# Fused hashed attention and gated attention experts: the scale chain in a bank, signs from two-byte halves, a first pair in four-byte tiles

## The chip, the cores and the metric

The kernel runs on one core of one Trainium2 chip. The metric is the device time of one execution in microseconds (us). The engines are PE (matrix multiplication, with PEld for its weight loads), DVE (vector), ACT (scalar and activation), POOL (GpSimd) and SP, whose queue issues every DMA of this kernel.

## The reference

Two stages. Stage one is attention within hash buckets, for 4 batches of 8 heads; stage two is a gated mixture of 4 causal attention experts on what stage one returns.

```python
q_bits = (np.einsum('bhsd,dk->bhsk', q, proj) > 0)      # B, H, S, D = 4, 8, 768, 64; proj is 64 x 6
k_bits = (np.einsum('bhsd,dk->bhsk', k, proj) > 0)
mask = q_bucket[:, :, :, None] == k_bucket[:, :, None, :]   # bucket: the 6 bits as a number
scores = np.where(mask, scale * q @ k.T, -1e9)              # scale = 1 / 8
attn = exp(scores - max); attn /= attn.sum() + 1e-9
x = (attn @ v) as (B, S, H * D)
# then, for each of 4 experts e, of which the gate takes 2 per token:
a = softmax(causal(scale * (x @ wq[e]) @ (x @ wk[e]).T))
out += gate weight * (a @ (x @ wv[e]) @ wo[e])
```

## The kernel before

**Units.** The work is cut into units: ("L", b, h) is one head of stage one, ("M", b, e) one expert of stage two, 48 in all. The first eight units are the heads of batch 0; after that heads of batch b stand between experts of batch b-1. Heads come in pairs (hp), and a pair is prepared together: 16 pairs.

**One head.** `max_steps` multiplies queries by keys into the bank `mx`, nine chunks of up to 512 columns, and DVE takes the maxima of each into `pm`. `shift_steps` folds them to `negm`, transposes that on PE, and DVE makes `row`, the shift of each query; a DMA puts it into the rows of `qa` behind the data. `s_unit` then multiplies again, keys by queries into bank `st`, ACT takes the exponential twice (`p` in four bytes, `ph` in two), POOL subtracts to get the rest `pl`, and PE multiplies by the values into bank `o`. `normalise` divides (`rden`) into `xp`.

**Halves.** Numbers of four bytes are multiplied as a sum of two-byte halves: `qa` and `ka` hold the high half, `qb` and `kb` a mixture of high and low halves, so that two matmuls give the product. The halves are first scaled by a power of two, found from the largest absolute value of the pair (columns 0, 1 and 2 of the tile `cs` for queries, keys and values; in the first pair `cqk`).

**Preparing a pair.** `scales` (run as `pair_scales`): DVE reduces queries, keys and values of the pair (`mqk`); `scale_of` spreads the result over partitions by matmuls into a bank of the ring `misc`, and a chain of seven or eight small DVE instructions on tiles `cmax` and `cs` makes the scales. `prep_pair`: PE transposes queries and keys into `misc`; each transposed bank is read three times, into `Tq` or `Tk` (four bytes, unscaled), into `qa` or `ka` (scaled), and for the rest into `qb` or `kb`. `bits` multiplies `Tq` and `Tk` by the projection `pbd` as four-byte matmuls, four groups of 32 columns side by side; DVE makes zero or one less a constant (`m`), ACT scales it (`M`), and DMAs put it into the rows of `qa` and `ka` behind the 64 rows of data. Equal buckets give a shift that unequal ones do not have. `halves` copies the parts of `qb` and `kb` by DMA. The first pair is prepared head by head, with scales of its own, and `split_first` for the head that is needed first.

**Shared places.** `misc` is a ring of two banks, used by scales, transposes, projections, row shifts and outputs alike. `mx` has two banks, `st` three, `o` one. While PE has nothing to do at the start it multiplies `ident` into `o`, to no purpose but its clock.

**Order.** Operations are recorded and then ordered by a list scheduler in the kernel itself: it has a table of costs (`_cost`), priorities by kind of work (`PRIO`), and for copies two engines to choose from (`choose`, `copy`). Each engine then runs its list in that order; nothing overtakes.

Every operation is issued from one helper, so all rows of the profile bear one line number; they are told apart by tile names.

Of the kernel before, what the change touches and what calls it, by code (L numbers as in the profile page):

```python
# [117 lines left out]
class Ring:  # L118
# [4 lines left out]
    def ready(self, c):  # L123

        if not self.loose and self.todo[self.next] is not c:
            return None
        if len(self.done) < self.bufs:
            return 0.0
        old = self.done[-self.bufs]
        return old.end if old.left == 0 else None  # L130
# [10 lines left out]
PRIO = {"norm": -300, "pair_scales": -300}  # L141
# [18 lines left out]
def _cost(rec, eng, name, out, ins, args, kw):  # L160
# [43 lines left out]
class Recorder:  # L204
# [100 lines left out]
    def schedule(self):  # L305
# [27 lines left out]
        while left:  # L333
            left -= 1
            best = None
            for e, lst in cand.items():
                t0 = free[e]
                pick = None
                for o in lst:
                    r = o.ready[e]  # L340
                    ok = True
                    for c in o.new:
                        if not c.placed:
                            x = c.ring.ready(c)
# [82 lines left out]
BIG = 2.0 ** 120  # L427
LN_SHIFT = 5.545177444479562
# [7 lines left out]
FIRST = {("v", 0): "m0", ("q", 1): "m"}  # L436
P1 = -3
W0 = 2
# [6 lines left out]
def tile_kernel(ctx, tc, q, k, v, proj, w_gate, wq, wk, wv, wo, out):  # L445
# [37 lines left out]
    for nm, src in (("q", q), ("k", k)):  # L483
        NAT[nm, 0, 0] = sb.tile([128, 2, NT, D], FT, name="nat" + nm, bufs=2)
# [33 lines left out]
    pat = con.tile([1, 2, 128], BF, name="pat")  # L518
# [3 lines left out]
    nc.gpsimd.memset(pat[:, 1], MISS)  # L522
    for g in range(4):
# [3 lines left out]
        else:  # L527
            nc.gpsimd.memset(pat[:, 0, o:o + 2 * NB], 1.0)
            nc.gpsimd.memset(pat[:, 0, o + 2 * MR:o + 2 * MR + 4], -1.0)
            nc.gpsimd.memset(pat[:, 1, o + 2 * MR:o + 2 * MR + 4], UNIT)  # L530
    pp = misc()
    for i in range(2):
        nc.tensor.matmul(pp[:, i:i + 1], pat[:, i], one16[:, 0:1], start=True, stop=True)
    sub_mul = con.tile([128, 2], FT, name="sub_mul")
    nc.vector.tensor_copy(sub_mul, pp[:, 0:2])
# [24 lines left out]
    PM = [con.tile([128, NT, 4], FT, name=f"pm{i}") for i in range(3)]  # L560
    lower = con.tile([2 * NT, 1], FT, name="lower")
# [69 lines left out]
    def spare(name="st", bufs=3):  # L631

        return psum.tile([128, 512], FT, name=name, bufs=bufs)

    def scale_of(mxs, c, to=12, bank=None):

        n = len(mxs)
        p = (bank or misc)()
# [7 lines left out]
        nc.vector.tensor_scalar(c.bitcast(I32), c.bitcast(I32), -1, float((127 + to + 127) << 23),  # L646
                                op0=OP.mult, op1=OP.add)

# [4 lines left out]
    def scales(b, hp, hs, nats, sc):  # L653

        early = not (b or hp)
        n = len(nats)
        m = sb.tile([128, 3], FT, name="mqk", bufs=2)[:, 0:n]
        if (b, hp) == (0, 1):
            nc.gate = marks["m"]
        for i, nat in enumerate(nats):  # L660
            nc.vector.tensor_reduce(m[:, i:i + 1], nat[:, hs[0]:hs[-1] + 1].rearrange("p h j d -> p (h j d)"),
                                    axis=AX.X, op=OP.max, apply_absolute_value=True)
            if i < n - 1 and not early:
                yield 0
        nc.gate = None
        c = sb.tile([128, 5], FT, name="cqk") if early else CS[b % 2][:, hp]
        scale_of([m[:, i:i + 1] for i in range(n)], c[:, 0:n], 10, spare if early and not hs[0] else None)
        nc.vector.tensor_scalar(c[:, 3:4].bitcast(I32), c[:, 0:1].bitcast(I32), -1, float((127 + 19 + 127) << 23),
                                op0=OP.mult, op1=OP.add)
        marks["c", b, hp] = nc.vector.tensor_tensor(c[:, 1:2], c[:, 1:2], c[:, 3:4], op=OP.min)  # L670
        nc.vector.tensor_scalar(c[:, 3:4], c[:, 0:1], c[:, 1:2], D ** 0.5, op0=OP.mult, op1=OP.mult)
        nc.vector.reciprocal(c[:, 4:5], c[:, 3:4])
        for h in hs:
            sc[h] = c
        yield 213

    def pair_scales(b, hp):
        sc = {}
        yield from scales(b, hp, [0, 1], [NAT[nm, b, hp] for nm in "qkv"], sc)
        SC[b, hp] = sc  # L680
        done.add(("sc", b, hp))

    def prep_pair(b, hp):
# [9 lines left out]
        TT = {nm: sb.tile([128, 2, HS], FT, name="T" + nm, bufs=1) for nm in "qk"}  # L693
        m0 = sb.tile([128, HS], HF, name="m0", bufs=1)
        M = sb.tile([128, HS], HF, name="M", bufs=1)
        sc = SC[b, hp] if (b, hp) in SC else {}
        early = not (b or hp)

        def bits(gs, parts):
            p = spare() if early and 0 in gs else misc()  # L700
            for g in gs:
                nc.tensor.matmul(p[32 * g:32 * g + 32, :HS], pbd, TT["q" if g < 2 else "k"][:, g % 2], start=True,
                                 stop=True, tile_position=(0, 32 * g))
            for r in parts:
                nc.vector.tensor_scalar(m0[r], p[r, :HS], 0.0, sub_mul[r, 0:1], op0=OP.is_gt, op1=OP.subtract)
                marks["m"] = nc.scalar.activation(M[r], m0[r], AF.Copy, scale=sub_mul[r, 1:2])
            for g in gs:
                a, n = (ds[g % 2]["qa"], MR) if g < 2 else (ds[g % 2]["ka"], MR + 2)
                nc.sync.dma_start(a[D:D + n].rearrange("p (j s) -> p j s", j=2),
                                  M[32 * g:32 * g + 2 * n][:, None, :])  # L710

        def transposed(nm, h):
            p = spare("mx", 2) if early and not h else misc()
            nc.gate = None if early else marks["c", b, hp]
# [4 lines left out]
            nc.copy(TT[nm][:, h], p[:, :HS], bias=C0)  # L719
            return p  # L720

        def split(nm, h, p):
            d = ds[h]
            c = sc[h][:, 0:1] if nm == "q" else sc[h][:, 1:2]
            d["scale"] = sc[h][0:1, 4:5]
            a, r = (d["qa"], d["qb"][:, od]) if nm == "q" else (d["ka"], d["kb"][:, ev])
            nc.copy(a[:, ev], p[:, :HS], c, bias=C0)
            marks["t"] = nc.vector.scalar_tensor_tensor(r, p[:, :HS], c, a[:, ev], op0=OP.mult, op1=OP.subtract)
            marks["a"] = nc.sync.dma_start(a[lo, od], a[hi, ev])

        def split_first(nm, p):

            d = ds[0]
            c = sc[0][:, 0:1] if nm == "q" else sc[0][:, 1:2]
            d["scale"] = sc[0][0:1, 4:5]
            a, r = (d["qa"], d["qb"][:, od]) if nm == "q" else (d["ka"], d["kb"][:, ev])
            nc.copy(a[lo, ev], p[lo, :HS], c[lo], bias=C0)
            nc.copy(a[lo, od], p[hi, :HS], c[hi], bias=C0)
            t = sb.tile([128, HS], HF, name="th", bufs=2)
            nc.copy(t, p[:, :HS], c, bias=C0)  # L740
            marks["t"] = nc.vector.scalar_tensor_tensor(r, p[:, :HS], c, t, op0=OP.mult, op1=OP.subtract)

        if early:
            for h in range(2):
                while h and step[0] < -2:
                    yield 0
                if h:
                    for _ in scales(b, hp, [h], [nats[nm] for nm in "qk"], sc):
                        pass
                ps = {nm: transposed(nm, h) for nm in "qk"}  # L750
                if not h:
                    bits((0, 2), [slice(32 * g, 32 * g + 32) for g in (0, 2)])
                    marks["m0"] = marks["m"]
                    for _ in scales(b, hp, [h], [nats[nm] for nm in "qk"], sc):
                        pass
                for nm in "qk":
                    if h:
                        split(nm, h, ps[nm])
                    else:
                        split_first(nm, ps[nm])  # L760
                if h:
                    bits((1, 3), [slice(32 * g, 32 * g + 32) for g in (1, 3)])
# [616 lines left out]
```

## Time and profile before

| | us |
|---|---|
| runs, median of 3 (lowest to highest) | 726.29 (725.09 to 726.68) |
| profiled execution, its own time | 723.28 |
| its span, first to last instruction | 721.5 |
| PE busy / PEld busy | 670.3 / 516.1 |
| DVE busy / ACT busy / POOL busy | 553.2 / 524.1 / 468.9 |
| mean granted clock of PE | 0.985 |

Busy time is a sum over stages: the start, the eight heads of batch 0, the mixture of heads and experts, and the last experts have different limits. `o<-ident` counts as busy at the start and is no work.

### The profile page before, as it was taken

How to read it: one execution, taken by the hardware profiler on the slowest of the kernel's cores; microseconds unless marked ns; L12 is line 12 of the kernel's file. 1: busy time of each engine (PE TensorE's matmuls, PEld its weight loads, DVE VectorE, ACT ScalarE, POOL GpSimd, SP SyncE). 2: the span in 40 equal slices, each digit the busy share in tenths (PEclk: the TensorE clock that was granted, in tenths of full speed). 3: DMA queues.
4: the chain of work that ended last, by engine and by line, in shares of the span. 5: the costliest groups of instructions: out<-in, count | busy, mean ns of one | idle time of the engine just before them, and what ended most of it. 6: DMA issues, size and time to landing. Idle time of an engine off the chain costs nothing.

```text
span 721.5 us, 21617 instructions
## 1 busy us (share of the span) xinstructions
PE 670.3 (93%) x8306; PEld 516.1 (72%) x8306; DVE 553.2 (77%) x1328; ACT 524.1 (73%) x1109; POOL 468.9 (65%) x490
## 2 busy tenths in 40 slices
PE   7977898889899998989999999989999899999997
PEld 6755566656777777668877777757877678788885
DVE  5968899998978878798668888688867867626652
ACT  3295588886787876987776887777777687962674
POOL 3085689786676885876656795776555596980453
PEclk9998899999999999999999999999999999999999
DMA  4322533324233132325115132224214121001122
GB/s 91 86 62 64 111 83 89 69 67 95 75 72 80 27 89 50 74 55 124 48 63 121 24 72 69 60 58 92 72 72 96 44 51 41 3 3 45 45 89 89
DMA packets 109782, 49.05 MB, mean 68 GB/s; under 512 B 88432, under 2 KB 106352, under 8 KB 109680
## 3 DMA queue, kind: packets, MB, share of 16 engines
q1 hardware_dynamic: 109680, 47.68, 27.4%
q8 instruction: 65, 1.06, 0.7%
q14 instruction: 37, 0.30, 0.2%
HBM read 20.98 MB, written 6.29 MB: 38 GB/s over the span
## 4 chain that ended last, share of the span: by engine, by line
PE 51%; DVE 26%; DMA 8%; ACT 8%; issue 4%; SPq 3%; POOL 0%; ACTq 0%; DVEq 0%; POOLq 0%
PE misc L422 19%; PE st L422 13%; PE o L422 11%; DVE pm L422 10%; PE mx L422 7%; DMA natv<-in_v_dram 4%; SPq L422 3%; DVE cs L422 3%; ACT ph L422 2%; ACT p L422 2%; DVE cmax L422 2%; DVE mqk L422 2%; DMA ot<-in_moe_wk_dram 1%; DVE kb L422 1%; DVE ka L422 1%
## 5 line engine op out<-in xcount | busy, mean ns | idle before, releaser
L422 POOL TENSOR_TENSOR pl<-p,ph 128x512 f16<-128x512 f32 (+2 forms) x384 | 424.8, 1128 | 210.1 <-ACT ph L422 113.5
L422 DVE TENSOR_REDUCE pm<-mx 128x2 f32<-128x512 f32 (+3 forms) x416 | 251.7, 623 | 33.9 <-PE mx L422 30.0
L422 ACT ACTIVATE p<-st 128x512 f32<-128x512 f32 (+2 forms) x386 | 235.5, 610 | 55.4 <-PE st L422 50.9
L422 ACT ACTIVATE ph<-st 128x512 f16<-128x512 f32 (+2 forms) x384 | 234.9, 613 | 0.5 <-PE o L422 0.4
L422 PEld LDWEIGHTS <-ph 128*128 128x128 f16 x2976 | 154.7, 98 | 32.9 <-issue 10.0
L422 PE MATMUL st<-qa,ka 78*128 78x256 f16 (+5 forms) x512 | 161.8, 325 | 7.2 <-ACT ph L422 4.8
L422 PE MATMUL st<-qb,kb 128*128 128x256 f16 (+3 forms) x512 | 160.1, 324 | 0.0
L422 PE MATMUL mx<-ka,qa 76*128 76x256 f16 (+5 forms) x512 | 143.4, 326 | 18.0 <-DVE pm L422 12.8
L422 PEld LDWEIGHTS <-pl 128*128 128x128 f16 x1488 | 136.8, 98 | 12.4 <-POOL pl L422 5.7
L422 PE MATMUL o<-vh,ph 128*128 128x65 f16 x1152 | 126.1, 194 | 1.8 <-DVE xp L422 1.6
L422 PE MATMUL o<-vh,pl 128*128 128x65 f16 x1152 | 125.0, 194 | 2.1 <-POOL pl L422 1.8
L422 PE MATMUL o<-vl,ph 128*128 128x64 f16 x1152 | 125.0, 192 | 0.0
L422 PEld LDWEIGHTS <-kb 128*128 128x128 f16 x512 | 50.6, 99 | 31.8 <-issue 14.9
L422 PEld LDWEIGHTS <-qa 76*128 76x128 f16 (+1 forms) x512 | 47.0, 99 | 36.0 <-issue 14.8
L422 PEld LDWEIGHTS <-ka 78*128 78x128 f16 (+1 forms) x512 | 50.5, 99 | 16.1 <-issue 6.5
L422 PEld LDWEIGHTS <-ident 128*128 128x128 bf16 x486 | 39.5, 103 | 14.2 <-issue 4.0
L422 ACT ACTIVATE qa<-misc,qkc 128x384 f16<-128x384 f32 x29 | 16.8, 580 | 34.6 <-PE misc L422 34.6
L422 PE MATMUL o<-mvh,ph 128*128 128x65 f16 x336 | 37.2, 197 | 1.8 <-DVE yn L422 0.9
L422 PE MATMUL o<-mvh,pl 128*128 128x65 f16 x336 | 37.0, 197 | 0.0
L422 PE MATMUL o<-mvl,ph 128*128 128x64 f16 x336 | 36.9, 196 | 0.0
L422 POOL TENSOR_TENSOR vl<-cv,vh 128x384 f16<-128x384 f32 x32 | 28.1, 885 | 10.9 <-ACT vh L422 6.5
L422 DVE SCALAR_TENSOR_TENSOR kb<-misc,qkc,qa 128x384 f16<-128x384 f32 x32 | 19.5, 610 | 18.1 <-ACT qa L422 18.1
(210 smaller groups left out, 1156.6 us busy)
## 6 DMA issues: line engine op xcount, KB each, us to landing
natv<-in_v_dram SPq DMA_DIRECT2D x16, 384.0 KB
natq<-in_q_dram SPq DMA_DIRECT2D x15, 384.0 KB
natk<-in_k_dram SPq DMA_DIRECT2D x15, 384.0 KB
out_dram<-ot SPq DMA_DIRECT2D x20, 256.0 KB
qb<-qa SPq DMA_DIRECT2D x48, 96.0 KB
kb<-ka SPq DMA_DIRECT2D x48, 96.0 KB
qb<-qb SPq DMA_DIRECT2D x32, 48.0 KB
kb<-kb SPq DMA_DIRECT2D x32, 48.0 KB
```

Of the source, the lines that this page charges most:

```text
L422: getattr(getattr(self.nc, e), m)(*[real(x) for x in args], **{k: real(x) for k, x in kw.items()})
```

## The change

Five things, in one diff:

1. `scale_of` and `pair_scales` keep the intermediate results of the chain (largest value, its exponent, two products) in free columns of the `misc` bank into which the matmuls wrote, in place of `cmax` and columns of `cs`. The instructions are as many; the bank is held until the last of them. The work of `pair_scales` has priority -100 in place of -300, `shift_steps` gets -100, `halves` +50.
2. For pairs 2 to 16 the signs come from the halves: the projection is scaled and split into `pbh` and `pbl` (`proj_halves`, once), and three groups of four two-byte matmuls, of 32 columns each, replace four four-byte ones. `Tq` and `Tk` are not made any more, and the signs wait for the halves.
3. The first pair (`prep_first`) is held in four-byte tiles, in the buffers `xth` and `xtl`, unscaled but for the factor 1/8 at the queries. No scale is found for it. Its products are single-pass four-byte matmuls, its DMAs move twice the bytes, its row shift is one row, its exponential needs no scale register.
4. The second pair's scale is found from queries and keys alone; its values get a scale of their own in `prep_v`.
5. Loads of the second and third pair's data are gated by other events (`FIRST`, `P1`).

```diff
-PRIO = {"norm": -300, "pair_scales": -300}
+PRIO = {"norm": -300, "pair_scales": -100, "shift_steps": -100, "halves": 50}
-FIRST = {("v", 0): "m0", ("q", 1): "m"}
+FIRST = {("k", 1): "m", ("v", 1): "row", ("q", 2): "m", ("k", 2): "m"}
...
+    pbh = con.tile([128, 32], HF, name="pbh")
+    pbl = con.tile([128, 32], HF, name="pbl")
...
-        t = sb.tile([128, 3], FT, name="cmax")[:, 0:n]
+        t, e = p[:, 384:384 + n], p[:, 388:388 + n]
         nc.vector.tensor_reduce(t, p[:, 0:128 * n].rearrange("p (a b) -> p a b", a=n), axis=AX.X, op=OP.max)
         nc.vector.tensor_scalar(t, t, 1e-30, None, op0=OP.max)
-        nc.vector.tensor_scalar(c.bitcast(I32), t.bitcast(I32), 0x7F800000, None,
-                                op0=OP.bitwise_and)
-        nc.vector.tensor_scalar(c.bitcast(I32), c.bitcast(I32), -1, float((127 + to + 127) << 23),
+        nc.vector.tensor_scalar(e.bitcast(I32), t.bitcast(I32), 0x7F800000, None, op0=OP.bitwise_and)
+        nc.vector.tensor_scalar(c.bitcast(I32), e.bitcast(I32), -1, float((127 + to + 127) << 23),
                                 op0=OP.mult, op1=OP.add)
...
+        u, w = p[:, 392:393], p[:, 393:394]
+        marks["c", b, hp] = nc.vector.tensor_tensor(c[:, 1:2], u, c[:, 1:2], op=OP.min)
+        nc.vector.tensor_scalar(w, c[:, 0:1], c[:, 1:2], D ** 0.5, op0=OP.mult, op1=OP.mult)
+        nc.vector.reciprocal(c[:, 4:5], w)
...
+    def prep_first():
+        ...
+        for nm, h in [("q", 0), ("k", 0), ("q", 1), ("k", 1)]:
+            ...
+            nc.copy(T[:, h], p[:, :HS], bias=C0)
+            nc.copy(a[:, ev], p[:, :HS], 0.125 if nm == "q" else None, bias=C0)
+            ...
+            if nm == "k":
+                p = misc()
+                ...
+                    nc.tensor.matmul(p[32 * g:32 * g + 32, :HS], pbd, TT["q" if g < 2 else "k"][:, h], start=True,
+                                     stop=True, tile_position=(0, 32 * g))
+                signs(p, gs, ds, [slice(32 * g, 32 * g + 32) for g in gs], M, 2, 1)
...
+    def proj_halves():
+        ...
+        scale_of([mx], c[:, 0:1])
+        t = sb.tile([128, 32], FT, name="pbs", bufs=1)
+        nc.scalar.activation(t, pbd, AF.Copy, scale=c[:, 0:1])
+        nc.scalar.activation(pbh, t, AF.Copy)
+        nc.gpsimd.tensor_tensor(pbl, t, pbh, op=OP.subtract)
...
-            nc.copy(TT[nm][:, h], p[:, :HS], bias=C0)
...
+        for n, (w, x) in enumerate(((pbh, 0), (pbl, 0), (pbh, 1))):
+            for g in range(4):
+                nc.tensor.matmul(p[32 * g:32 * g + 32, :HS], w, parts[g][x], start=not n, stop=n == 2,
+                                 tile_position=(0, 32 * g))
+        signs(p, range(4), ds, [slice(0, 128)], sb.tile([128, HS], HF, name="M", bufs=1), 1, 2)
...
-        if not (b or hp):
+        if not b and hp < 2:
             mx = sb.tile([128, 1], FT, name="mx")
...
+            row = sb.tile([NT, 128], FR, name="roww", bufs=1)
+            marks["row"] = nc.vector.tensor_scalar(row, p[0:NT, 0:128], LN_SHIFT, None, op0=OP.add)
```

How it stands in the lists of the engines, at three places.

The first place is DVE at the start of the program, behind the copy of `sub_mul`. Before (`m` are the signs, `cmax` and `cqk` the scale of the first pair):

```order
L422 TENSOR_REDUCE mqk<-natq 128x1
L422 TENSOR_REDUCE mqk<-natk 128x1
L422 COPY pbd<-pst 64x6 x4
L422 TENSOR_SCALAR m_216<-st,sub_mul 32x384 x2
L422 TENSOR_REDUCE cmax<-st 128x2
L422 TENSOR_REDUCE mqk<-natq 128x1
L422 TENSOR_SCALAR cmax<-cmax 128x2
L422 TENSOR_REDUCE mqk<-natk 128x1
L422 TENSOR_SCALAR cqk<-cmax 128x2
L422 TENSOR_SCALAR cqk<-cqk 128x2
```

And now (`xth` and `xtl` are the buffers of the four-byte `qa`, `qb` and `ka`, `kb`, `pmw` the maxima):

```order
L423 TENSOR_SCALAR xth<-misc 128x384
L423 COPY pbd<-pst 64x6 x4
L423 SCALAR_TENSOR_TENSOR xth<-misc,xth 128x384
L423 TENSOR_TENSOR xtl<-misc,xtl 128x384
L423 TENSOR_SCALAR m_231<-misc,sub_mul 32x384 x2
L423 COPY Tq<-misc 128x384
L423 TENSOR_SCALAR xth<-misc 128x384
L423 CAST xtl<-misc 128x384
L423 SCALAR_TENSOR_TENSOR xth<-misc,xth 128x384
L423 TENSOR_TENSOR xtl<-misc,xtl 128x384
L423 TENSOR_SCALAR m_311<-misc,sub_mul 32x384 x2
L423 TENSOR_REDUCE pmw_151<-mx 128x2 x6
```

The scale of the first pair is gone from the list, and both heads are prepared before the first maximum is taken.

The second place is SP where the row shift of the fourth head is issued. Before (`ot` are staging tiles of the expert weights):

```order
L422 DMA ot<-in_moe_wq_dram 128x4x64
L422 DMA ot<-in_moe_wk_dram 128x4x64
L422 DMA natv<-in_v_dram 128x12x64
L422 DMA qb<-qa 64x768
L422 DMA kb<-ka 64x768
L422 DMA qa<-row 2x6x128
L422 DMA fq_110<-fr 2x6x128
```

And now:

```order
L423 DMA ka<-M 14x2x384 x2
L423 DMA qa<-row 2x6x128
L423 DMA fq_113<-fr 2x6x128
L423 DMA ot<-in_moe_wq_dram 128x4x64
L423 DMA ot<-in_moe_wk_dram 128x4x64
L423 DMA natv<-in_v_dram 128x12x64
```

The row shift stands ahead of two weight loads and of a load of values, where it stood behind them.

The third place is DVE at the scale chain of the third pair. Before:

```order
L422 TENSOR_REDUCE cmax<-misc 128x3
L422 TENSOR_REDUCE pm_144<-mx 128x2
L422 TENSOR_SCALAR cmax<-cmax 128x3
L422 TENSOR_REDUCE pm_144<-mx 128x2
L422 TENSOR_SCALAR cs_665<-cmax 128x3
L422 TENSOR_REDUCE pm_144<-mx 128x2
L422 TENSOR_SCALAR cs_665<-cs_665 128x3
```

And now, from the reduction of the same pair on:

```order
L423 TENSOR_REDUCE misc<-misc 128x3
L423 TENSOR_REDUCE negm_143<-pm_149 128x12
L423 TENSOR_REDUCE pm_145<-mx 128x2
L423 TENSOR_SCALAR misc<-misc 128x3
L423 TENSOR_REDUCE pm_145<-mx 128x2
L423 TENSOR_SCALAR misc<-misc 128x3
L423 SCALAR_TENSOR_TENSOR row<-misc,up 12x128
L423 TENSOR_SCALAR cs_524<-misc 128x3
L423 TENSOR_REDUCE pm_145<-mx 128x2
L423 TENSOR_SCALAR misc<-cs_524 128x1
```

The chain's operands are in the bank, and `negm` and `row` of the head ahead stand between its steps.

More of the change, by code (lines that the diff above doesn't have):

```diff
@@ L121, in __init__, with ready @@
         self.todo, self.next, self.done = [], 0, []
-    def ready(self, c):
-        if not self.loose and self.todo[self.next] is not c:
-            return None
-        if len(self.done) < self.bufs:
+    def ready(self, c, k=0):
+        if not self.loose and self.todo[self.next + k] is not c:
+            return None
+        n = len(self.done) + k - self.bufs
+        if n < 0:
             return 0.0
-        old = self.done[-self.bufs]
+        old = self.done[n]
         return old.end if old.left == 0 else None
@@ L341, in schedule @@
                     ok = True
-                    for c in o.new:
+                    for i, c in enumerate(o.new):
                         if not c.placed:
-                            x = c.ring.ready(c)
+                            x = c.ring.ready(c, sum(d.ring is c.ring for d in o.new[:i]))
                             if x is None:
@@ L427 @@
 BIG = 2.0 ** 120
+WIDE = 2.0 ** 60
 LN_SHIFT = 5.545177444479562
@@ L467, in raw, with move @@
         return ap.bitcast(FT)
+    def move(to, of):
+        nc.sync.dma_start(*[raw(x) if x.dtype == FR else x for x in (to, of)])
     NAT, marks = {}, {}
@@ L560, in tile_kernel @@
     PM = [con.tile([128, NT, 4], FT, name=f"pm{i}") for i in range(3)]
+    PMW = [con.tile([128, NT, 4], FT, name=f"pmw{i}") for i in range(2)]
     lower = con.tile([2 * NT, 1], FT, name="lower")
@@ L566, in tile_kernel @@
         nc.gpsimd.memset(t, -CLIP)
+    for t in PMW:
+        nc.gpsimd.memset(t, -WIDE / 2)
     nc.gpsimd.memset(lower, 1.0 / UNIT)
@@ L647, in scale_of @@
+        nc.vector.tensor_scalar(c.bitcast(I32), e.bitcast(I32), -1, float((127 + to + 127) << 23),
                                 op0=OP.mult, op1=OP.add)
+        return p
     SC = {}
[L653 to L664, printed above, removed]
-        nc.gate = None
[L666 to L681, printed above, removed]
+    def pair_scales(b, hp):
+        second = (b, hp) == (0, 1)
+        while second and "t" not in marks:
+            yield 0
+        m = sb.tile([128, 3], FT, name="mqk", bufs=2)
+        names = "qk" if second else "qkv"
+        for i, nm in enumerate(names):
+            nc.gate = marks[GS] if second else None
+            nc.vector.tensor_reduce(m[:, i:i + 1], NAT[nm, b, hp].rearrange("p h j d -> p (h j d)"), axis=AX.X, op=OP.max,
+                                    apply_absolute_value=True)
+            nc.gate = None
+            yield 0
+        c = CS[b % 2][:, hp]
+        n = len(names)
+        p = scale_of([m[:, i:i + 1] for i in range(n)], c[:, 0:n], 10)
+        u, w = p[:, 392:393], p[:, 393:394]
+        nc.vector.tensor_scalar(u.bitcast(I32), c[:, 0:1].bitcast(I32), -1, float((127 + 19 + 127) << 23),
+                                op0=OP.mult, op1=OP.add)
+        marks["c", b, hp] = nc.vector.tensor_tensor(c[:, 1:2], u, c[:, 1:2], op=OP.min)
+        nc.vector.tensor_scalar(w, c[:, 0:1], c[:, 1:2], D ** 0.5, op0=OP.mult, op1=OP.mult)
+        nc.vector.reciprocal(c[:, 4:5], w)
+        SC[b, hp] = c
+        done.add(("sc", b, hp))
+        yield 330
@@ new lines, in signs @@
+    def signs(p, gs, ds, parts, M, mul, rows):
+        m0 = sb.tile([128, HS], HF, name="m0", bufs=1)
+        for r in parts:
+            nc.vector.tensor_scalar(m0[r], p[r, :HS], 0.0, sub_mul[r, 0:1], op0=OP.is_gt, op1=OP.subtract)
+            marks["m"] = nc.scalar.activation(M[r], m0[r], AF.Copy, scale=sub_mul[r, mul:mul + 1])
+        for g in gs:
+            a, n = (ds[g % 2]["qa"], MR) if g < 2 else (ds[g % 2]["ka"], MR + rows)
+            move(a[D:D + n].rearrange("p (j s) -> p j s", j=2), M[32 * g:32 * g + 2 * n][:, None, :])
@@ new lines, in proj_halves @@
+    def proj_halves():
+        while "row" not in marks:
+            yield 0
+        mx = sb.tile([128, 1], FT, name="mx")
+        nc.gate = marks["row"]
+        nc.vector.tensor_reduce(mx, pst, axis=AX.X, op=OP.max, apply_absolute_value=True)
+        nc.gate = None
+        c = sb.tile([128, 2], FT, name="cscale", bufs=6)
+        scale_of([mx], c[:, 0:1])
[3 more added lines that the diff above has]
+        nc.gpsimd.tensor_tensor(pbl, t, pbh, op=OP.subtract)
+        done.add("pb")
+        yield 109
@@ L692, in prep_pair @@
         nats = {nm: NAT.pop((nm, b, hp)) for nm in "qk"}
[L693 to L714, printed above, removed]
+        c = SC.pop((b, hp))
+        parts = []
+        for nm, h in [("q", 0), ("q", 1), ("k", 0), ("k", 1)]:
+            d = ds[h]
+            d["scale"] = c[0:1, 4:5]
+            cn = c[:, 0:1] if nm == "q" else c[:, 1:2]
+            a, r = (d["qa"], d["qb"][:, od]) if nm == "q" else (d["ka"], d["kb"][:, ev])
+            p = misc()
+            nc.gate = marks["c", b, hp]
             for t in range(NT // 2):
@@ L731, in split_first @@
[L731 to L762, printed above, removed]
-                yield 436 * (NT // 2)
-        else:
-            for nm, h in [("q", 0), ("q", 1), ("k", 0), ("k", 1)]:
-                split(nm, h, transposed(nm, h))
-                yield 109 * (NT // 2)
-            bits(range(4), [slice(0, 128)])
+            nc.copy(a[:, ev], p[:, :HS], cn, bias=C0)
```

117 lines of the change are left out of this document (77 added, 40 removed).

## The prediction

> **What bounds the kernel now.** I read the busy times by stretch first, since one average hides four stages.
>
> ```profile
> 0.00:33.00 33.00, 29.02 (x331) 24.34 (x332) 24.27 (x56) 8.87 (x16) 5.93 (x48) 0.95 0.40 89
> 33.00:100.00 67.00, 56.73 (x680) 38.64 (x677) 55.26 (x126) 48.36 (x101) 44.95 (x41) 0.92 0.34 77
> 100.00:165.00 65.00, 57.08 (x771) 39.48 (x772) 60.67 (x132) 56.25 (x121) 54.77 (x50) 1.00 0.35 78
> 165.00:665.00 500.00, 475.92 (x6001) 372.36 (x6002) 387.06 (x939) 376.75 (x800) 339.04 (x327) 0.99 0.27 64
> 665.00:721.50 56.50, 51.53 (x528) 41.25 (x525) 25.94 (x78) 33.87 (x74) 24.25 (x24) 0.99 0.21 71
> ```
>
> Columns are length, then busy PE, PEld, DVE, ACT, POOL, the granted clock, DMA. Until 33 us nothing useful but preparation runs (PE's busy time there is mostly idle multiplication of `ident`). From 33 to 100 no engine is full: the stages wait for each other. From 100 to 165 DVE bounds, 60.67 of 65. From 165 to 665 PE does, 475.92 of 500: only 24 us of idle PE can be won there. The last 56 us hold no pair preparation.
>
> **The head of the program (term A).** I followed the chain of waits to the first product into `st`, and took its steps from the timeline.
>
> ```profile
> 4.22 0.85 PE L422 MATMUL mx<-ident,natq 128*128 128x128 f32 x3
> 6.39 0.49 ACT L422 ACTIVATE Tk<-mx 128x384 f32<-128x384 f32 x1 [0.79 <-PE mx L422]
> 9.29 1.25 DVE L422 TENSOR_SCALAR m<-st,sub_mul 32x384 f16<-32x384 f32 x2 [3.42 <-PE st L422]
> 10.57 0.99 SPq L422 DMA_DIRECT2D qa<-M  x1
> 11.60 0.88 SPq L422 DMA_DIRECT2D ka<-M  x1
> 16.45 0.10 PEld L422 LDWEIGHTS <-qa 76*128 76x128 f16 x1 [1.91 <-ACT th L422]
> 28.08 0.20 DVE L422 TENSOR_REDUCE negm<-pm 128x12 f32<-128x48 f32 x1
> 29.76 0.27 DVE L422 SCALAR_TENSOR_TENSOR row<-misc,up 12x128 f16<-12x128 f32 x1
> 30.88 0.67 SPq L422 DMA_DIRECT2D qa<-row  x1
> 33.12 0.38 PE L422 MATMUL st<-qa,ka 78*128 78x512 f16 x1
> ...
> L422 DVE CAST xth<-misc 128x384 fp32r<-128x384 f32 x8 | 4.4, 556 | 3.8 <-PE misc L422 3.8
> L422 DVE TENSOR_REDUCE pm<-mx 128x2 f32<-128x512 f32 x320 | 212.0, 680 | 27.7 <-PE mx L422 24.0 <-PE o L422 2.0
> L422 DVE TENSOR_REDUCE mqk<-natq 128x1 f32<-128x768 f32 x15 | 14.2, 944 | 5.9 <-DMA natq<-in_q_dram 5.9
> L422 DVE COPY pbd<-pst 64x6 f32<-64x6 f32 x4 | 1.2, 561 | 0.0
> ```
>
> (The last four rows are groups: count, busy, mean ns.) Between the signs at 10.5 and the first maximum at 17 stands the scale of the first head and its halves: the load at 16.45 waits for ACT `th`. Without it I lay DVE's new list on these durations. Queries are transposed at 5.07; copy 0.56, projection 1.2, two residuals of 0.6: 8.0. The key copies on ACT are done at 6.88 + 0.49 = 7.4, so they are beside this. Signs of 1.25 end at 9.3, 1.2 earlier than 10.54; so do their DMAs, 12.48 - 1.2 = 11.3, and a landing of some 1.8 (row DMA issued 30.88 to 31.55, used at 33.12: 1.6) gives 13.1. Meanwhile DVE prepares the second head: 0.55 + 4 x 0.57 + 1.25 = 4.1, to 13.4. Then ten `pm` at 0.65 net of overlap and one `mqk` to the end of `negm`: 7.7, at 21.3 instead of 28.28. Two more `pm` and an `mqk` stand ahead of the row: it ends at 23.8 instead of 30.03, and SP's queue is empty then, so the first `st` comes near 26.7, some 6 us earlier. The four-byte DMAs (twice the bytes) are issued before 18 and have 8 us to land. Four-byte matmuls of 512 columns are under the 0.68 of `pm`, which takes them one by one.
>
> ACT then gets stuck once: it has the value scale behind five of nine chunks, which DVE makes after all maxima of the second head, at about 34.6 by the same sum, so two of the 6 us are lost and regained, since `Tq` and `Tk` of the next pair no longer stand between its exponentials. Further along:
>
> ```profile
> 65.87 0.27 DVE L422 SCALAR_TENSOR_TENSOR row<-misc,up 12x128 f16<-12x128 f32 x1
> 69.84 0.63 PE L422 MATMUL st<-qa,ka 78*128 78x512 f16 x1
> 83.07 0.27 DVE L422 SCALAR_TENSOR_TENSOR row<-misc,up 12x128 f16<-12x128 f32 x1
> 85.76 0.72 SPq L422 DMA_DIRECT2D qa<-row  x1
> 88.27 0.38 PE L422 MATMUL st<-qa,ka 78*128 78x512 f16 x1 [0.48 <-DMA qa<-row]
> 88.49 0.38 PE L422 MATMUL st<-qb,kb 128*128 128x512 f16 x1
> 64.00:71.00 7.00, 3.89 (x19) 2.08 (x18) 5.97 (x16) 2.84 (x7) 1.77 (x2) 0.82 0.09 23
> 71.00:77.00 6.00, 6.00 (x36) 2.87 (x35) 4.11 (x8) 4.38 (x9) 2.85 (x3) 0.64 0.65 138
> ```
>
> The third head's `st` is at 69.84, held by its pair's preparation. Continued, the sum puts that row at 60 and its `st` near 63: **A = -7** (-4 if the landings are slow, -9 if ACT does not stall).
>
> **SP's queue (B).** The fourth head's row is ready at 83.34 but issued at 85.76, behind weights and values; PE waits for it at 88.27. Now it stands ahead of them: **B = -2.4** (0 to -2.5). What is late next is the weight load, which feeds experts only after 165.
>
> **The clock (C).** After the idle stretch at 64 to 71 the clock was 0.64 for 6 us of full PE: 2.2 us lost. A shorter gap saves part: **C = -1** (0 to -2).
>
> **The scale chain (D).** From the groups by shape:
>
> ```profile
> L422 DVE TENSOR_SCALAR cmax<-cmax 128x3 f32<-128x3 f32 x15 | 7.9, 528 | 0.1
> L422 DVE TENSOR_SCALAR cs<-cmax 128x3 int32<-128x3 int32 x15 | 8.0, 532 | 0.1
> L422 DVE TENSOR_SCALAR cs<-cs 128x3 int32<-128x3 int32 x15 | 5.3, 355 | 0.1
> L422 DVE TENSOR_TENSOR cs<-cs 128x1 f32<-128x1 f32 x15 | 6.3, 417 | 0.0
> L422 DVE RECIPROCAL rden<-rden 128x6 f32<-128x6 f32 x32 | 5.9, 184 | 0.5
> L422 DVE RECIPROCAL gm<-misc 128x6 f32<-128x6 f32 x4 | 0.8, 192 | 0.1
> L422 DVE TENSOR_TENSOR rden<-o,gw 128x6 f32<-128x6 f32 x16 | 2.5, 156 | 0.2
> ```
>
> Three values per partition should not take half a microsecond; twice as many out of a bank take 0.156. At 0.16 each the four save 0.37 + 0.37 + 0.19 + 0.26 = 1.2 us per pair, 18 us of DVE over 15 pairs. They lie on the path only where DVE is late. The copies into `Tq` and `Tk` go too:
>
> ```profile
> L422 ACT ACTIVATE Tq<-misc 128x384 f32<-128x384 f32 x23 | 10.8, 494 | 12.5 <-PE misc L422 9.8 <-DVE qa L422 2.5
> L422 ACT ACTIVATE Tk<-misc 128x384 f32<-128x384 f32 x20 | 10.0, 501 | 9.3 <-DVE ka L422 4.9 <-PE misc L422 4.2
> L422 DVE COPY Tk<-misc 128x384 f32<-128x384 f32 x11 | 6.0, 545 | 0.6 <-PE misc L422 0.4
> L422 DVE COPY Tq<-misc 128x384 f32<-128x384 f32 x8 | 4.3, 535 | 0.2 <-PE misc L422 0.2
> ```
>
> That is 62 copies for 16 pairs, of which the first keeps four: some 20 us of ACT and 10 of DVE. So DVE loses about 1.8 us per pair. A pair is prepared for every two heads, and in the 65 us that DVE bounds four to five heads pass, so two pairs, 3.6 us: **D = -3** (-1 to -5).
>
> [...]
>
> **Signs on PE (E).**
>
> ```profile
> 46.22 0.52 PE L422 MATMUL misc<-Tq,pbd 128*32 128x384 f32 x2
> 46.56 0.49 PE L422 MATMUL misc<-Tq,pbd 128*32 128x384 f32 x2
> ```
>
> The four groups start together, and each has two passes 0.34 apart: 0.7 us of PE per pair. Two-byte matmuls of 512 columns follow each other in 0.22 (88.27 and 88.49), so 384 columns take 0.165, and three rounds of four side by side 0.5. 15 x 0.2: **E = -3** (-4 to -1). Without overlap it would be 12 x 0.165 = 2.0 per pair.
>
> **The PE-bound middle (F).** Ten pairs lie there. Chain and copies leave 18 us less on DVE and some 13 on ACT, beside PE that is idle 24 us, part of which waits for DVE. I take one sixth of the idle time, being nearer to nothing than to all since PE fills most gaps with other heads: **F = -4** (-9 to 0).
>
> **What it costs (G).** The bank is held through the chain; 72 products of the first two heads become four-byte, beside DVE that sets their pace; `proj_halves` adds a dozen short instructions. **G = +2.5** (0 to +4).
>
> Sum: -7 - 2.4 - 1 - 3 - 3 - 4 + 2.5 = -17.9. The profiled execution of 723.28 (span 721.5 and 1.8 around it) becomes 705.4. The median of the runs lies 3.0 above that execution, so for a median I say 708.4.
>
> **Rivals.**
>
> *Only the head wins.* PE fills the rest with the same work, D and F come to nothing: A + B + C or less, -3 to -10, 716 to 723. For it speaks PE's 95% after 165; against it, that DVE is full from 100 to 165.
>
> *The small instructions keep their half microsecond* because it is not where the operands lie. Then D and F halve, and time is near 712 to 716. Against it: the spread, 0.16 from the bank as above. [...]
>
> *The held bank makes it slower.* From the spreading matmuls to the reciprocal a chain with other DVE work between its steps holds one of two `misc` banks, some 5 to 7 us where maxima (0.68 each) stand between. Projections and outputs then go through one bank: each waits for a read of 0.5 to 0.6 (`xth` above). Three such in each of 15 pairs cost 15 x 3 x 0.55 = 25 us if PE has nothing else, 726 + 25 - 18 = 733. It decides the sign once two thirds of these waits are uncovered. Against it: the lists put heads' products into that span, and each transposed bank is read twice where it was read three times.
>
> *The groups of four do not overlap in two bytes:* 15 x (2.0 - 0.7) = +19 in place of -3, 708 + 22 = 730. Against it: four-byte ones overlap.
>
> **Chances.** Forecast (697 to 713) 0.70; only the head 0.12; small instructions keep their price 0.05; held bank 0.06; no overlap 0.04; within 0.2% (what a measurement of this kernel can tell from no change) otherwise 0.03. Faster 0.87, same 0.03, slower 0.10. The forecast's own range is the sum of favourable and unfavourable ends, cut where several must meet: 697 to 713; with the two smaller gains, 697 to 722, which leaves the last three cases and the tail below 697 outside, under 2 in 10.
>
> **What would show it.** First `st` near 27; third head's `st` near 63; row DMAs of the fourth head not after weights; `misc<-misc` of 128x3 at 0.15 to 0.2; no `Tq` past the first pair; twelve sign products within 0.7 us; PE idle between 165 and the same place under 22. The prediction is wrong if the stretch to the last head of batch 0 shrinks by under 8, or if waits of PE and ACT for `misc` grow past 20 us.

## The result, and the profile after

The kernel after takes 679.38 us (median of 4 runs, 677.2 to 679.66) beside 725.69 for the kernel before on the same chip (723.89 to 726.68): a ratio of 0.9358, interval 0.933 to 0.9386. That is 46 us less where 18 were forecast; 708 was said, and 697 was the lower end. The profiled execution of after took 679.66 us, with a span of 676.8.

The busy times by stretch, cut where the same units end (the third row ends with the eighth head, before at 165.3; the last row covers all of the middle at once). Columns are length, PE, PEld, DVE, ACT, POOL, clock, DMA:

```profile
0.00:27.00 27.00, 24.20 (x301) 20.91 (x302) 20.07 (x42) 5.58 (x9) 6.20 (x53) 1.00 0.54 117
27.00:82.50 55.50, 49.81 (x654) 37.28 (x652) 44.54 (x108) 45.47 (x96) 43.29 (x41) 1.00 0.47 101
82.50:145.40 62.90, 58.88 (x832) 42.71 (x830) 58.54 (x145) 54.75 (x117) 55.22 (x52) 1.00 0.38 86
145.40:621.00 475.60, 464.42 (x6051) 371.62 (x6050) 366.27 (x917) 369.17 (x786) 339.28 (x328) 1.00 0.29 67
621.00:676.80 55.80, 50.18 (x516) 40.01 (x514) 24.62 (x74) 34.14 (x74) 24.34 (x24) 0.98 0.21 72
...
145.40:613.80 468.40, 457.22 (x5992) 364.89 (x5991) 360.77 (x902) 367.67 (x782) 339.28 (x328) 1.00 0.29 67
```

The same middle in the kernel before, from the end of the eighth head to the unit that ends at 613.8 after:

```profile
165.30:656.00 490.70, 467.96 (x5942) 365.56 (x5935) 379.87 (x919) 374.52 (x796) 338.70 (x326) 0.99 0.27 64
```

Up to the eighth head 19.9 us are gained (165.3 to 145.4), in the middle 22.3 (490.7 to 468.4), behind it 2.5. In the middle PE's idle time fell from 22.7 to 11.2, and its busy time, for the same units, by 10.7. Signs account for about 2 of that and half clock for some 3. The rest, some 5, may be short waits that the records count as busy; no run shows this. So the 24 us of idle time on which the prediction put a ceiling were not all that could be won there.

The places that the prediction named, from the timeline of after:

```profile
27.25 0.48 PE L423 MATMUL st<-xth,xtl 77*128 77x512 f32 x1
...
56.33 0.27 DVE L423 SCALAR_TENSOR_TENSOR row<-misc,up 12x128 f16<-12x128 f32 x1
59.05 0.38 PE L423 MATMUL st<-qa,ka 78*128 78x512 f16 x1
64.80 0.34 PE L423 MATMUL misc<-qa,pbh 128*32 128x384 f16 x2
65.40 0.39 PE L423 MATMUL st<-qb,kb 128*128 128x512 f16 x1
71.07 0.66 SPq L423 DMA_DIRECT2D qa<-row  x1
...
72.46 0.40 SPq L423 DMA_DIRECT2D ot<-in_moe_wq_dram  x1
74.58 0.51 SPq L423 DMA_DIRECT2D natv<-in_v_dram  x1
```

The first `st` is at 27.25 (26.7 was worked out), the third head's at 59.05 (63), and the fourth head's row goes out ahead of weights and values. The twelve sign products hold PE from 64.80 to 65.40: 0.60 us.

The scale chain, in the groups of DVE (count, busy, mean ns):

```profile
L423 DVE TENSOR_SCALAR misc<-misc 128x3 f32<-128x3 f32 x14 | 2.2, 156 | 0.0
L423 DVE TENSOR_SCALAR misc<-misc 128x3 int32<-128x3 int32 x14 | 2.2, 156 | 0.0
L423 DVE TENSOR_SCALAR cs<-misc 128x3 int32<-128x3 int32 x14 | 2.1, 151 | 0.0
L423 DVE TENSOR_TENSOR cs<-misc,cs 128x1 f32<-128x1 f32 x15 | 2.2, 146 | 0.1
```

The four steps cost 0.15 to 0.16 us each, as forecast. The largest of PE's waits, first before, then after:

```profile
PE mx L422 <- DVE pm L422: 12.8, 22, 1.5
```

```profile
PE mx L423 <- DVE pm L423: 5.0, 13, 0.6
```

PE's waits for `misc`, added up over all their rows, fell too, from 12.8 to 3.8 us, and those of ACT from 84.0 to 73.4: no delay by the held bank shows.

### The profile page after: what moved, and what is told of

It is laid out like the page before. It is cut to its first block, busy times and chain, and to the rows that moved or that the text cites. A ratio compares the mean times of both kernels' runs of the same rounds, so it can differ in the third digit from the quotient of the medians.

```text
span 676.8 us, 21637 instructions
## 1 busy us (share of the span) xinstructions
PE 647.5 (96%) x8344; PEld 512.5 (76%) x8344; DVE 514.0 (76%) x1282; ACT 509.1 (75%) x1080; POOL 468.3 (69%) x496
## 4 chain that ended last, share of the span: by engine, by line
PE 67%; DVE 16%; DMA 7%; ACT 4%; issue 3%; POOL 2%; SPq 1%; ACTq 0%; POOLq 0%; DVEq 0%
PE misc L423 24%; PE st L423 17%; PE o L423 16%; PE mx L423 9%; DVE pm L423 8%; DMA natv<-in_v_dram 4%; ACT ph L423 2%; DMA ka<-M 1%; SPq L423 1%; ACT p L423 1%; POOL pl L423 1%; DVE mqk L423 1%; DVE misc L423 1%; DVE kb L423 1%; DMA qb<-qb 1%
## 5 line engine op out<-in xcount | busy, mean ns | idle before, releaser
L423 ACT ACTIVATE p<-st 128x512 f32<-128x512 f32 (+2 forms) x386 | 231.8, 600 | 67.2 <-PE st L423 64.0
L423 DVE TENSOR_REDUCE pm<-mx 128x2 f32<-128x512 f32 (+3 forms) x398 | 239.1, 621 | 34.0 <-PE mx L423 31.9
L423 ACT ACTIVATE ph<-st 128x512 f16<-128x512 f32 (+2 forms) x384 | 230.2, 603 | 1.0 <-PE o L423 1.0
L423 PE MATMUL st<-qa,ka 78*128 78x512 f16 (+1 forms) x488 | 152.3, 322 | 5.7 <-ACT ph L423 3.8
L423 PE MATMUL st<-qb,kb 128*128 128x512 f16 x488 | 151.2, 321 | 0.0
L423 PE MATMUL mx<-ka,qa 76*128 76x512 f16 (+1 forms) x488 | 133.7, 322 | 7.3 <-DVE pm L423 3.7
L423 PEld LDWEIGHTS <-qa 76*128 76x128 f16 (+1 forms) x488 | 43.9, 98 | 28.4 <-issue 10.2
L423 PEld LDWEIGHTS <-ka 78*128 78x128 f16 (+1 forms) x488 | 47.7, 98 | 15.3 <-issue 5.4
L423 PEld LDWEIGHTS <-ident 128*128 128x128 bf16 x469 | 35.8, 100 | 14.7 <-issue 5.2
L423 PE MATMUL misc<-xth,wqk_h 128*128 128x384 f32 x128 | 32.6, 370 | 0.1
```

The lines of the kernel that those rows point to most:

```text
L423: getattr(getattr(self.nc, e), m)(*[real(x) for x in args], **{k: real(x) for k, x in kw.items()})
```

## The experiments

Two numbers are used beside the time. The granted clock of each run gives what half clock took: span times (1 - clock). What is left, span times clock, is the time at full clock. Both are means over the runs of a kernel; half clock in which nothing waits for PE is counted too, so what it took is an upper bound of what it cost.

**1. The chain back in SBUF, order unchanged.** Every list stands instruction for instruction as in after; the planner sees the bank, the instructions get a tile.

```diff
         t, e = p[:, 384:384 + n], p[:, 388:388 + n]
+        t.alias, e.alias = side[:, 0:n], side[:, 4:4 + n]      # side: an SBUF tile of 128x16
...
         u, w = p[:, 392:393], p[:, 393:394]
+        u.alias, w.alias = p.side[:, 8:9], p.side[:, 9:10]
```

> The kernel after, with every instruction of every engine in the same place of its list; only the intermediate values of the scale chain (largest value, exponent, two products) lie in an SBUF tile again and not in the bank. Theory 1, VectorE's relief by the short chain is what lets TensorE run: the chain instructions go back to 0.35 to 0.55 us, VectorE's busy time rises by some 18 us, and the time goes to 692 to 702 us, most of it lost between unit 8 and the end of the mixture, where TensorE's idle time doubles. Theory 2, the order (new priorities, new plan) is what did it: VectorE's busy time rises by as much, but the time stays within 4 us of 679.4. Rival on the operands, the half microsecond was not a matter of where they lie: the chain stays at 0.15 to 0.2 us and nothing changes.

702.82 us, ratio to before 0.9685 (0.9644 to 0.9726). The chain's groups are back where they were:

```profile
L432 DVE TENSOR_SCALAR cs<-cside 128x3 int32<-128x3 int32 x14 | 8.9, 639 | 0.0
L432 DVE TENSOR_SCALAR cside<-cside 128x3 f32<-128x3 f32 x14 | 7.8, 554 | 0.0
L432 DVE TENSOR_TENSOR cs<-cside,cs 128x1 f32<-128x1 f32 x15 | 5.7, 377 | 0.1
L432 DVE TENSOR_SCALAR cside<-cside 128x3 int32<-128x3 int32 x14 | 5.0, 359 | 0.0
```

DVE's busy time rises by 20 us (514.0 to 534.2) and the time by 23 (the mean span by 24.5, of which 16 at full clock and 8.5 by half clock). So where the operands lie is the cause of the half microsecond, and it comes back as time about one for one, though DVE is idle for a quarter of the span. The time is just above the 692 to 702 of theory 1. The expectation had most of it in the middle; 12 of the 23 were lost by the end of the eighth head. One place shows how. Engines of the timeline of this kernel:

```profile
298.22 5.63 POOL L432 TENSOR_TENSOR pl<-p,ph 128x512 f16<-128x512 f32 x5
...
300.73 3.15 DVE L432 TENSOR_SCALAR cside<-cside 128x3 f32<-128x3 f32 x1
303.80 0.68 DVE L432 TENSOR_REDUCE pm<-mx 128x2 f32<-128x512 f32 x1
...
304.53 0.31 PE L432 MATMUL mx<-ka,qa 76*128 76x256 f16 x1 [2.81 <-DVE pm L432]
```

A step on three values per partition takes 3.15 us. It ends at 303.88, when POOL's row of five subtractions ends (298.22 + 5.63 = 303.85). The maximum behind it on DVE is late, and PE waits 2.81 us for it. The same step in after:

```profile
284.60 0.15 DVE L423 TENSOR_SCALAR misc<-misc 128x3 f32<-128x3 f32 x1
284.67 0.67 DVE L423 TENSOR_REDUCE pm<-mx 128x2 f32<-128x512 f32 x1
```

And what the wait brought, by windows of this first experiment:

```profile
301.20:304.60 3.40, 0.59 (x6) 0.35 (x5) 3.40 (x4) 1.43 (x3) 2.65 (x3) 1.00 0.01 2
304.60:308.00 3.40, 3.40 (x37) 2.53 (x37) 2.61 (x13) 1.25 (x3) 1.15 (x1) 0.50 0.02 6
```

Behind a window with 0.59 us of PE work stands one at half clock. In the kernel before, too, PE waits behind such steps. Around its largest one, where no half clock followed:

```profile
121.99 1.28 POOL L422 TENSOR_TENSOR wqk_l<-ot,wqk_h 128x512 fp32r<-128x512 f32 x1
122.33 2.08 DVE L422 TENSOR_SCALAR cmax<-cmax 128x3 f32<-128x3 f32 x1
123.22 1.17 POOL L422 TENSOR_TENSOR pl<-p,ph 128x512 f16<-128x512 f32 x1
124.33 0.54 DVE L422 TENSOR_TENSOR xp<-o,rden 128x384 f32<-128x384 f32 x1
124.92 0.19 PE L422 MATMUL o<-vh,ph 128*128 128x65 f16 x1 [1.58 <-DVE xp L422]
```

Small DVE instructions of scales on SBUF that took over 0.3 us: 30 in before, 34 in this kernel, and each of these 64 ends within 0.03 us of the end of a POOL instruction. They are `tensor_scalar` on two or three columns and `tensor_tensor`; `tensor_scalar` on one column (53 and 55 of them) and `reciprocal` on one column (22 and 20) never took over 0.3. That POOL holds such a step up is read from these ends; by what it does so is not shown. The step of 3.15 us is longer than any one of the five subtractions (1.13 each), so it got no turn between them. That is the exception: three of the 64 lasted through more than one POOL instruction (3.15 here, 2.08 and 1.70 in before), and 35 ended where the next POOL instruction began at once.

**2. Old priorities; 3. old signs (in after).** Each planned anew.

```diff
-PRIO = {"norm": -300, "pair_scales": -100, "shift_steps": -100, "halves": 50}
+PRIO = {"norm": -300, "pair_scales": -300}
```

> The kernel after with the two priorities of before (300 ahead for the scales and the normalisation, none for row shifts and halves); everything else as it is, the plan is made anew. Theory 2 (order): 690 to 705 us, the loss in the mixture. Theory 1 (VectorE's relief): within 4 us of 679.4, since all short instructions stay.

701.21 us, ratio 0.9644 (0.9603 to 0.9686). This is theory 2's range, as experiment 1 came out near theory 1's: both the operands and the order count, and each by over 20 us once the rest is there. The time at full clock rises by 9 us, the loss by half clock by 14. The clock of the profiled run:

```profile
core 0: 701.4 us, clock 0.976
```

```diff
+            nc.copy(TT[nm][:, h], p[:, :HS], bias=C0)
...
-                nc.tensor.matmul(..., w, parts[g][x], ...)     # 3 x 4, two bytes
+            nc.tensor.matmul(..., pbd, TT["q" if g < 2 else "k"][:, g % 2], ...)     # 4, four bytes
```

> The kernel after with the signs of pairs 2 to 16 made again from four-byte copies of the transposed data (Tq, Tk) by four four-byte products; the projection's halves are still made, and unused. Theory 3, the copies on ScalarE and VectorE were what held TensorE up: 690 to 700 us. Theory 1 alone (chain): 3 to 6 us slower than 679.4, that is 682 to 686, of which 3 are the products on TensorE.

695.77 us, ratio 0.9594 (0.9545 to 0.9644): theory 3's range. PE needs 0.2 us more per pair, 3 in all; the other 13 fall to the copies, 18 us of ACT and 13 of DVE in this kernel, and to the new plan, whose luck experiments 5 and 17 put at 2 to 7.

**4. All but the first pair.** The kernel before with chain, signs and priorities.

```diff
+        t, e = p[:, 384:384 + n], p[:, 388:388 + n]      # chain in the bank, as in the change
...
+            for n, (w, x) in enumerate(((pbh, 0), (pbl, 0), (pbh, 1)) if TT is None else ()):      # all but the first pair
...
+PRIO = {"norm": -300, "pair_scales": -100, "shift_steps": -100, "halves": 50}
```

> The kernel before with the chain in the bank, the signs from the two-byte halves and the new priorities, but with its old first pair, old gates of the loads and old scale of the second pair's values. If the middle gains by these parts alone and the start by the first pair alone, the end of the eighth head stays late (some 158 to 163 us) and the time is 692 to 700 us. If the start's gain also sets the middle's (order, clock), it is over 705 us.

687.28 us, ratio 0.9466 (0.9421 to 0.9511), and the eighth head ends at 151.9: both lower than either case of the expectation. So 39 of the 46 us come without the new first pair.

**5, 6, 17. Nudged plans.** Each shifts a margin of the planner that means nothing on the chip.

```diff
-RING = 200.0
+RING = 190.0      # 5 in after, 6 in before; 17, in after: WAIT 75 to 80
```

> The kernel after with one number of the planner nudged that stands for nothing on the chip (the margin it leaves behind a ring's release, 200 to 190 ns), which puts a tenth of the instructions elsewhere in their lists. Theory 4, any new plan costs some 15 to 20 us because this one happened to fit, and so the losses of 22 and 16 us with the old priorities and the four-byte signs say little of either: 690 to 700 us. Theory 5, the plan's details are worth a few microseconds and the losses were those of the parts: 676 to 685 us.

> The kernel before with the same nudge of the planner (200 to 190). Theory 5: within 5 us of 726. Theory 4, plans scatter by 15 us: anywhere from 710 to 740 us.

> The kernel after with another number of the planner nudged that stands for nothing on the chip (the margin for a signal, 75 to 80 ns). If this plan is a lucky one among plans that scatter by some 7 us: 683 to 690 us again. If the first nudge was the unlucky one: 677 to 682 us.

After: 686.86 and 681.78 us, 2 to 7 over 679.4, the first between the ranges of theories 4 and 5. Before: 726.27, ratio 1.0008 (0.9977 to 1.0039), no change. So this plan of after is a fitting one, by 2 to 7 us, and a loss of that size by another edit says nothing of the edit.

**7, 8, 10, 11, 12, 18. The parts alone and in pairs, on the kernel before.** The edits are the three pieces of experiment 4's diff, one or two at a time.

> The kernel before with the scale chain kept in the bank and nothing else; planned anew. If the chain's 1.2 us per pair comes back one for one, as it did when it was put back into SBUF in the kernel after (19 us of VectorE, 23 us of time): 702 to 710 us. If it was worth so much only beside the other parts: 715 to 722 us, which is what the prediction's terms D and F allowed (7 us). If the held bank costs: over 726 us.

> The kernel before with the signs of pairs 2 to 16 from the two-byte halves (no Tq and Tk for them, twelve two-byte products a pair) and nothing else; planned anew. By the sum of the prediction (3 us on TensorE, 1.6 of the copies where VectorE bounds, some of F): 718 to 722 us. If the copies' 20 us of ScalarE and 10 of VectorE come back as time as the chain's did: 700 to 712 us.

> The kernel before with the new priorities alone. The kernel before with chain, signs and priorities took 687.3 us, with the chain alone 718.8, with the signs alone 719.5. If the parts add up (in span times granted clock: 710 before, -6 chain, -10 signs, 682 all three), the priorities alone give 697 there and 708 to 714 us. If they count only once VectorE has room: 720 to 728 us.

> The kernel before with chain and signs, and the old priorities. If the parts add up: 710 - 16 = 694 of span times clock, and 703 to 711 us. If each hides the other's gain until both are gone: 690 to 700 us. If they win the same idle time: 714 to 719 us.

> The kernel before with the chain in the bank and the new priorities, and its old signs. If the parts add up: 703 to 709 us. If the chain pays in full only with the new priorities (the kernel after loses 23 us when its chain goes back to SBUF): 694 to 702 us.

> The kernel before with the signs from the two-byte halves and the new priorities, and its old chain in SBUF. Alone they gave 6 and 12 us. If they add up: 705 to 709 us. If the signs too pay more beside the new priorities, as the chain did (30 with them where 6 and 12 were had alone): 695 to 703 us.

| kernel | median us | ratio to before (interval) | full clock | half clock took |
|---|---|---|---|---|
| before (beside 5 to 8) | 725 | | 710.2 | 12.8 |
| chain | 718.76 | 0.9928 (0.990 to 0.9957) | 704.5 | 13.2 |
| signs | 719.49 | 0.9926 (0.9885 to 0.9968) | 700.7 | 17.1 |
| priorities | 713.04 | 0.9858 (0.9813 to 0.9902) | 707.4 | 3.9 |
| chain, signs | 710.27 | 0.975 (0.9671 to 0.9829) | 691.4 | 14.4 |
| signs, priorities | 698.50 | 0.9644 (0.9608 to 0.9679) | 693.3 | 3.0 |
| chain, priorities | 695.49 | 0.9613 (0.9553 to 0.9674) | 690.5 | 2.8 |
| all three | 687.28 | 0.9466 (0.9421 to 0.9511) | 681.8 | 3.8 |
| after | 679.38 | 0.9358 (0.933 to 0.9386) | 675.7 | 0.8 |

Each ratio is to runs of the kernel before on the same chip. From one such set to another, half clock took 11.4 to 13.7 us of the kernel before and full clock 709.3 to 710.7. The runs of chain with signs spread from 702 to 714, so that row is good to a few us only. Alone the parts give 6, 6 and 12 us, together 39. Two things make the difference. With the old priorities 13 to 17 us go to half clock, whatever else is done; with the new ones 3 to 4. And at full clock the chain gives 5.7 alone but 16.9 beside the priorities, the signs 9.5 alone and 14.1 beside them. Chain, signs and both together came in the ranges that add the parts up; each of them beside the priorities came in the range that has it pay more there. The expectation for the priorities named the right time for the wrong reason: it had all of it at full clock, but against the runs of before beside them (710.7 and 11.4) 7.5 of 10.8 us are half clock. How the order keeps the clock up is not shown.

**9. Idle products in the waits of before.**

```diff
+                for _ in range(FILLS.get(k, 0)):      # 37 places, 397 products, from the waits in the trace
+                    self.nc.tensor.matmul(bank[:, 400:512], ident, ident[:, 0:112], start=False, stop=False, ...)
```

> The kernel before with 397 idle products (ident into unused columns of the bank o) put into TensorE's list at 37 places ahead of 600 us, where it was seen to wait 0.35 us or more, each lot a little shorter than the wait; no other list changes. The waits themselves stay. If the half clock that follows a wait is a loss of its own: clock 0.992 to 1.0, and 8 to 13 us less than 725, that is 712 to 717 us. If half clock falls only where nothing is lost, or idle products change nothing: within 3 us of 725. If they stand in the way: over 728 us.

730.87 us, ratio 1.0092 (1.0063 to 1.0121): the products stand in the way. Against the runs of before beside it, the loss by half clock fell by 3 (11.4 to 8.1), but the time at full clock rose by 10. PE's busy time rose by 17 us and its idle time fell by 8 only, so about half of the products did not fit where the waits were. That a product there saves clock is shown; what the clock alone is worth is not.

**13 to 16. One priority at a time, in after.**

```diff
-PRIO = {"norm": -300, "pair_scales": -100, "shift_steps": -100, "halves": 50}
+PRIO = {"norm": -300, "pair_scales": -300, "shift_steps": -100, "halves": 50}      # 13; 14: shift_steps 0; 15: halves 0; 16: shift_steps -200
```

> The kernel after with the scales' priority alone back at 300 ahead. Undoing both old priorities cost 22 us, 14 of them by half clock; a nudge of the plan costs 7. If it is the scales, whose chain stood ahead of the maxima that TensorE waits for: 694 to 702 us with a clock under 0.985. If not: 676 to 688 us with a clock over 0.99.

> The kernel after with the row shifts' priority alone back at none. If it is the row shifts (an earlier row lets the next head's products into st start, so that TensorE has other work while a bank of mx is late): 692 to 702 us with a clock under 0.985. If not: 676 to 688 us.

> The kernel after with the halves' priority alone back at none. I hold it to be without effect: 676 to 688 us and a clock over 0.99. If the DMA queue's order is the cause: over 692 us.

> The kernel after with the row shifts 200 ahead in place of 100. If earlier rows are what keeps TensorE busy: 672 to 680 us, clock 1.0. If 100 was enough and the rest is the luck of the plan: 680 to 690 us.

Scales at 300: 691.42 us, half clock 4.0. Row shifts at 0: 692.38, half clock 5.0. Halves at 0: 687.34, half clock 4.8. Row shifts at 200: 681.44, half clock 2.4. The first lies between the two ranges of its expectation, and the second has the time of its first case without the low clock, so neither decides. None of the first three alone brings back the 15 us of half clock that experiment 2 shows with all three old numbers; the first two lose more time than the nudges do, the third about as much. Which of them does what stays open, and 200 for the row shifts is no better than 100.

The chain in the bank in the very order of before was not tried, so what it is worth there without a new plan is not known.

## Why the prediction was wrong

The direction held, and so did the cause of the half microsecond. The clock, the step from DVE's time to the path, and a missing term for the priorities are what failed. Put along one path of the table (priorities, then chain, signs, first pair), at full clock: -2.8, -16.9, -8.7, -6.1; half clock -12.0; together -46.5 in the mean span (723.0 to 676.5). Another path would share the sum out otherwise.

- **Head (A, B, G: -6.9).** Measured -6.1 at full clock for the first pair and the loads' gates. The first `st` came at 27.25 (26.7 said), the third head's at 59.05, four us earlier than said. But the sum agrees in part by luck: B is not of this step. With the priorities alone (experiment 10) the fourth head's row already goes out ahead of weights and values, at 80.83 in place of 85.76:

```profile
80.83 0.67 SPq L422 DMA_DIRECT2D qa<-row  x1
...
82.23 0.40 SPq L422 DMA_DIRECT2D ot<-in_moe_wq_dram  x1
83.54 0.50 SPq L422 DMA_DIRECT2D natv<-in_v_dram  x1
```

  So -6.1 stands against A and G, -4.5. G's cost does not show by itself.
- **Clock (C: -1, bounds 0 and -2): measured -12.0**, most of it by the priorities alone. This step failed. I took one burst at 64 to 77 us, since the page gives the clock in tenths of a slice, and did not ask what brings the half clock on; the mean clock of 0.985 in the table ahead of the prediction, over 721.5 us, says that up to 10.8 us were lost. Between 24 and 720 us before has bursts at 68.5, the one that I took, and at 89.0, 283.5 and 450.8 us, each behind a wait:

```profile
85.60:89.00 3.40, 1.48 (x7) 0.66 (x7) 2.82 (x6) 0.54 (x2) 1.26 (x1) 1.00 0.69 160
89.00:92.40 3.40, 3.40 (x15) 2.26 (x15) 3.05 (x9) 2.13 (x5) 1.15 (x1) 0.50 0.47 119
...
280.10:283.50 3.40, 1.92 (x13) 0.83 (x11) 3.40 (x13) 3.27 (x10) 2.07 (x3) 1.00 0.00 0
283.50:286.90 3.40, 3.38 (x47) 2.72 (x47) 2.63 (x8) 1.28 (x3) 1.84 (x3) 0.51 0.03 7
```

  Such a wait is paid a second time in the window behind it, where PE is full (3.40 and 3.38 of 3.40 us) and half as fast: in the burst at 89.0 two products of 512 columns into `st` follow each other in 0.42 us (91.02 and 91.44), where ahead of it they took 0.22 (88.27 and 88.49). And the waits ahead of the last two bursts come in good part from the chain itself. A step that POOL blocks (0.80 us, where it takes 0.14 at best; it ends at 282.76, and the POOL instructions beside it at 280.72 + 2.03 = 282.75) makes a maximum late, and PE waits 1.09 us for it:

```profile
281.96 0.80 DVE L422 TENSOR_TENSOR cs<-cs 128x1 f32<-128x1 f32 x1
282.76 0.67 DVE L422 TENSOR_REDUCE pm<-mx 128x2 f32<-128x512 f32 x1
283.48 0.57 PE L422 MATMUL mx<-ka,qa 76*128 76x512 f16 x1 [1.09 <-DVE pm L422]
```

  At 447.67 the same step takes 0.80 us again, and the same wait of 1.09 us follows, up to 449.20.
- **Chain, copies and middle (D and F: -7, with E's signs -10): measured -28.4 at full clock, priorities included.** DVE's saving was sized right (1.2 us per pair; 20 us of ACT and 10 of DVE for the copies), and so was E (0.79 to 0.60 us per pair, 2.8 in all). What failed is the step from DVE to the path: "one sixth of the idle time", out of a ceiling of 24 us. The mean of half a microsecond hid a spread: of the 30 blocked steps of before eight took over 1 us, and behind five of these PE waits for 0.5 to 1.6 us. Experiment 1 gives 16 us at full clock and 8.5 of half clock for the place of the chain's operands alone. And the ceiling counted recorded idle time only, while PE's busy time in the middle fell by 10.7 us as well.
- **Priorities: no term at all.** I showed in the lists that the order moved and priced only the row's DMA. Alone they give 12 us, and beside them the chain gives 16.9 at full clock in place of 5.7.
- **Rivals.** "Only the head wins" fell: without it 39 us remain. "Keeps its half microsecond" fell, by experiment 1. "Held bank" fell: waits for `misc` went from 12.8 to 3.8. "No overlap" fell: 0.60 us for twelve products.

## What to carry to other kernels

Before pricing a small instruction by its mean, read its spread, and see whether the long ones end together with another engine's instruction, as 64 of 64 did here within 0.03 us: the price of such a step is the wait of whoever stands behind it (2.81 us of PE behind the one of 3.15), not its duration. In a kernel whose engines run fixed lists, as here, parts that shorten the same waits can be worth little alone and much together, so undo them one at a time in the finished kernel as well as adding them to the old one, and nudge the plan to know what a new order costs by itself. Price a wait of TensorE with the half clock behind it, where the traces show one: here it followed 15 of 16 windows that were under 0.50 busy.

## What the chip showed that I had not expected

**Half clock follows a thin window, not an idle one.** Bursts of half clock last 3.41 us or a multiple (a last one is cut off by the end) and start on a grid of that step. In the profile of before they last 3.413, 6.827, 3.413, 3.413 and 3.413 us and start at 17.30, 68.50, 88.97, 283.53 and 450.79, each a whole number of steps of 3.413 behind the first. Laid over all 20 profiles (from 24 us on), with the share of the window in which the records have PE busy: under 0.50, 15 of 16 windows are followed by one at half clock; from 0.50 to 0.65, 43 of 84; above, 20 of 3821. A window without work was not needed: a wait of 1.09 us in a window 0.56 busy (280.10 above) was followed by half clock.

**The grid stood differently to the kernel in two runs.** Against the first instruction it is shifted by 0.2 us in the profile of before and by 0.8 in that of experiment 1 (bursts at 17.30 and 58.87, less whole steps of 3.413). In the 19 runs of before beside experiments 5 to 8 half clock took between 7.2 and 19.6 us. That the shift makes this difference is likely, but not shown.

**A DVE step that POOL blocks can miss the gap between POOL's instructions.** Most of the 64 blocked steps end with the POOL instruction that was running, but 3.15 us at 300.73 in experiment 1 and 2.08 and 1.70 us in before went on through two or three. What decides it is open.
